# First batch: the order in which pooled keys, v's weights, the last u column and the gate's low parts are made, and the opening of the second stage

## The chip, the cores and the metric

One core of a Trainium2 chip runs the whole program in one launch. The metric is the device time of one execution in microseconds (us). Five engines work side by side, each through a queue of its own in order: TensorE (PE; its weight loads are PEld), VectorE (DVE), ScalarE (ACT), GpSimd (POOL), and SyncE (SP), which issues the DMA transfers.

## The reference

Three layers follow each other, for 8 batches of 576 tokens with 512 features.

```python
k_p = k.reshape(B, H, Sp, 8, D).mean(axis=3); v_p = v.reshape(B, H, Sp, 8, D).mean(axis=3)
x = softmax(q @ k_p.T / sqrt(D)) @ v_p                  # 8 heads of 64, 72 pooled keys
h = gelu_tanh(x @ w_in); u, v = h[..., :512], h[..., 512:]
v_n = (v - mu) / sqrt(var + 1e-6) * g_ln                # per token
x2 = x + (u * (einsum('ts,bsd->btd', w_sg, v_n) + b_sg)) @ w_out
logits = x2 @ w_gate; top 2 of 4 experts, softmax weights
out = sum over the 2 experts of  w * (causal softmax(q k / 8) @ v @ wo)
```

All inputs are float32. The kernel keeps that precision on TensorE by splitting each operand into a high part (rounded to the format fp32r) and a low part (the rest), so that a product is three matmuls: high by high, high by low, low by high.

## The kernel before

The first stage, class PhaseA, takes each batch through pooled attention and the gated layer and writes x2 to DRAM. The second, class PhaseB, starts at 589.7 us of the span and takes each batch through the expert attention.

**First stage, one batch.** Keys and values are pooled by additions (pool_k L171, pool_v). For five tiles of tokens there are scores (sc, L224), the softmax (finish L247 divides by the sum and writes P), transposes (tr) and the product with the values (av). put_x splits the result: high part xh, low part xl, and a plain copy x32 for the sum at the end. Then come the columns of u (upart L407, four of them: U0 to U3), v (Y and V: 48 matmuls and a short fifth tile), the norm of v over its tokens (norm L379: statistics bs and mean and variance mv on VectorE, rs = 1/sqrt on GpSimd in L391 and L392, the high part vnh on ScalarE in L400, the low part vnl on VectorE in L402, for two tiles at a time), the product with w_sg (spatial, tile sp, four columns P0 to P3; L438 multiplies by u, L443 and L445 make the high part gh and the low part gl), and the product with w_out (outp L448, four columns f). L462 adds x32, ScalarE makes x2h and L464 the low part x2l. The two PSUM banks of the tag mm hold the columns of outp in turn, so column f + 2 cannot begin before L464 of column f is done.

**First batch.** It follows an order written by hand, the string SEQ, whose letters name steps in the table of first(). The steps run over a batch whose weights are still being made: W0 to W3 make the columns of w_in for u and W4 to W7 those for v, S0 to S5 those of w_sg, O0 to O3 those of w_out. W and O call load64 (L112), which takes a staged 64-bit load apart into a high and a low part: six VectorE instructions (L124, L125, L127 to L130) and two on ScalarE. load_ws (L156) subtracts the high from the loaded part of w_sg; the string SE says on which engine (P is GpSimd, D is VectorE). Within SEQ batch 1 is begun too: K, Q and o load its keys, its queries and w_out (the last and the raw keys and values share three buffers), k pools its keys, C, X and F are its scores, exponents and finish, R and v load and pool its values. FD lists the pairs (batch, tile) whose finish runs on VectorE, other pairs run on GpSimd. The step "k" before:

```python
def pool_k1():
    with after(4):
        self.pool_k(1)
```

after(4) means behind the finish of tile 4 of batch 0.

Engines take instructions in the order in which the scheduler puts them, which follows SEQ and the dependences. Nothing overtakes on an engine.

**Second stage.** proj makes q and k of a pair of experts in halves (items 00 to 03 are q, q, k, k of the first pair and 10 to 13 of the second), vproj the values (v0 to v4), gate the choice of the experts (g; L796 to L812 on VectorE). run() first does the items of PRE, then goes over units of scores: score (s), three units later trans (t, L886), and between them the items of the table FIRSTF for the first batch, FILL for the others.

Of the kernel before, what the change touches and what calls it, by code (L numbers as in the profile page):

```python
# [17 lines left out]
HS = S // 2  # L18
# [10 lines left out]
AXT = {(0, 0), (0, 2), (0, 4), (1, 0), (1, 2), (1, 3)}  # L29
FD = {(0, 0), (0, 1)}  # L30
XA = (0, 1, 2, 3)
VE = ('PPP', 'PPP')
KE = ('DD', 'PP')
SE = 'PDPP'
SEQ = ("a0 a1 b0 d0 b3 b1 b2 d1 b4 d2 c g p0 h0 h1 p1 h2 h3 s0 e0 f0 s1 e1 f1 s2 s3 e2 f2 e3 f3 "
       "s4 e4 f4 y0 y1 y2 t0 t1 t2 t3 t4 z l W0 U0 W1 U1 W2 U2 W3 U3 K Q k o0 o1 W4 Y0 W5 Y1 W6 Y2 W7 Y3 S2 S1 S0 "
       "V4 N0 S4 N2 S5 N4 S3 C0 C1 o2 O0 P0 C2 X0 X1 F0 o3 O1 P1 C3 F1 X2 O2 R P2 F2 X3 O3 "
       "P3 C4 F3 X4 v")
# [3 lines left out]
class PhaseA:  # L42
# [69 lines left out]
    def load64(self, tv, hi, lo):  # L112
# [16 lines left out]
        nc.vector.scalar_tensor_tensor(lf, zh, 2.0 ** 32, zl, op0=OP.mult, op1=OP.add)  # L129
        nc.vector.scalar_tensor_tensor(lo, lf, 2.0 ** -52, gf, op0=OP.mult, op1=OP.mult)  # L130

    def stage_wi(self, part, j):

        shape, tag = ([128, 2, 4, 128], "ws") if part == 0 else ([128, 2, 512], "wo")
        t = self.w.tile(shape, U64, tag=tag, name="st64", bufs=2)
        for i in range(2):
            k, s = self.wi_cols(part, 2 * j + i)
            self.nc.sync.dma_start(t[:, i], self.ins["w_in"][:, k, s])
            self.STG[part, 2 * j + i] = t[:, i]
# [141 lines left out]
    def av(self, b, steps):  # L281
# [8 lines left out]
        for x in steps:  # L290
# [15 lines left out]
            for p in range(NP):  # L306
                if p in done and "r" in done and (b, p) not in self.X32:
                    self.put_x(b, p, ps[p])

    def put_x(self, b, p, ps):  # L310
# [11 lines left out]
        nc.vector.tensor_sub(fh[:, S:], ps[:, 1, HS - 64:HS], fh[:, 512:S].bitcast(F32))  # L322
        if b == 0 and p in XA:
            nc.scalar.activation(x32, ps[:, :, :HS], AF.Copy)  # L324
        else:
            nc.gpsimd.tensor_add(x32, xh.bitcast(F32), xl.bitcast(F32))
# [80 lines left out]
    def upart(self, b, f):  # L407
# [3 lines left out]
        for h in range(2):  # L411
            s = slice(h * HS, h * HS + HS)
            o = ps[:, h, :HS]
            for kc in range(4):
                xh, xl = self.XH[b, kc][:, s], self.XL[b, kc][:, s]
                nc.tensor.matmul(o, self.wi[0][:, kc, c], xh, start=kc == 0, stop=False)  # L416
                nc.tensor.matmul(o, self.wi[0][:, kc, c], xl, start=False, stop=False)  # L417
                self.upmm = nc.tensor.matmul(o, self.wi[1][:, kc, c], xh, start=False, stop=kc == 3).ins  # L418
# [4 lines left out]
    def spatial(self, b, d):  # L423
# [19 lines left out]
        nc.scalar.activation(gh, u, AF.Copy)  # L443
        eng = nc.vector if d == 3 else nc.gpsimd
        eng.tensor_sub(gl, u, gh.bitcast(F32))  # L445
# [47 lines left out]
    def first(self):  # L493

        done = {}
        def after(i):
            return self.tc.issue_after(done[i]) if i in done else nullcontext()
# [6 lines left out]
        def pool_k1():  # L504
            with after(4):
                self.pool_k(1)
        def load_v1():
# [108 lines left out]
FILL = (('', '12 10 11', '', '13 x0 x1 x2 x3', '', '', 'o3 o1 o0', '', ''), ('v0', 'v1 00 02', '01 o2', '03', '', '', '', 'v2 v3', 'v4 g'))  # L616
FIRSTF = (('10', '11', '12', '13 x0 x1 x2 x3', '', '', '', '', ''), ('v0 00', '', '01 02 v1', '03', '', '', '', 'v2 v3', 'v4 g'))
LASTF = (('', '10 12 11', '', '', '13', '', 'o1', '', 'o0'), ('', '', '', '', '', 'o2', '', '', 'o3'))
SDF = {(0, 0), (0, 1), (0, 5), (0, 8), (1, 0), (1, 2), (1, 7)}
SDL = {(0, 4), (0, 6), (1, 6), (1, 7)}  # L620
PRE = 'v0 00 01 02 03 v1 v2 v3 v4 g'
AVS = [(0, 256), (256, S)]
# [393 lines left out]
```

## Time and profile before

| | us |
|---|---|
| median of 3 runs | 968.65 (967.56 to 971.37) |
| the profiled execution, its own time | 967.84 |
| its span in the trace | 966.1 |
| TensorE busy | 915.0 (95% of the span) |
| VectorE, ScalarE, GpSimd busy | 693.1, 519.0, 447.0 |

The span is counted from the first to the last instruction of the trace, 1.7 us less than the execution's own time. Busy time counts instructions, not register work, and a wait on a semaphore is put down to the instruction that ended it. On the page's 40 slices of 24 us TensorE is at 90% or more in all but the first five, slice 26 and the last. In a row of a time order the first number is the start, the second the duration, and a bracket gives the idle time ahead of it and what ended it.

### The profile page before, as it was taken

How to read it: one execution, taken by the hardware profiler on the slowest of the kernel's cores; microseconds unless marked ns; L12 is line 12 of the kernel's file. 1: busy time of each engine (PE TensorE's matmuls, PEld its weight loads, DVE VectorE, ACT ScalarE, POOL GpSimd, SP SyncE). 2: the span in 40 equal slices, each digit the busy share in tenths (PEclk: the TensorE clock that was granted, in tenths of full speed). 3: DMA queues.
4: the chain of work that ended last, by engine and by line, in shares of the span. 5: the costliest groups of instructions: out<-in, count | busy, mean ns of one | idle time of the engine just before them, and what ended most of it. 6: DMA issues, size and time to landing. Idle time of an engine off the chain costs nothing.

```text
span 966.1 us, 18451 instructions
## 1 busy us (share of the span) xinstructions
PE 915.0 (95%) x6488; PEld 864.4 (89%) x6488; DVE 693.1 (72%) x1869; ACT 519.0 (54%) x1285; POOL 447.0 (46%) x628
## 2 busy tenths in 40 slices
PE   4887699999999999999999999899999999999997
PEld 3677689989989999899899899799999999999987
DVE  6998557757667577577576514897878796878785
ACT  3755334344343343343443433677777777777776
POOL 6545847558369368376583560113222222323221
PEclk9797899999999999999999999999999999999999
DMA  9611522312402404223126014415253534435121
GB/s 326 236 35 44 172 80 82 121 61 71 157 25 81 160 13 140 99 65 132 56 61 191 25 39 134 140 37 176 61 172 88 162 94 147 118 108 163 49 61 75
DMA packets 51644, 102.86 MB, mean 106 GB/s; under 512 B 10592, under 2 KB 16736, under 8 KB 50656
## 3 DMA queue, kind: packets, MB, share of 16 engines
q1 hardware_dynamic: 51408, 101.68, 32.9%
q8 instruction: 52, 0.85, 0.4%
q14 instruction: 40, 0.33, 0.1%
q10 hardware_dynamic: 144, 0.00, 0.0%
HBM read 59.72 MB, written 28.31 MB: 91 GB/s over the span
## 4 chain that ended last, share of the span: by engine, by line
PE 63%; DVE 20%; ACT 6%; POOL 5%; issue 3%; DMA 2%; SPq 1%; POOLq 0%; ACTq 0%; DVEq 0%
PE av L906 4%; PE op L457 4%; PE op L458 4%; PE op L459 3%; PE sp L434 3%; PE sp L432 3%; PE sp L433 3%; PE sc L224 3%; PE t L886 3%; DVE vnl L402 3%; PE pj L715 2%; PE pj L713 2%; PE pj L714 2%; DVE vnh L404 2%; DVE bs L388 2%
## 5 line engine op out<-in xcount | busy, mean ns | idle before, releaser
L860 POOL TENSOR_SCALAR pr<-pr,sm,gw 128x128 f32<-128x128 f32 (+3 forms) x119 | 72.7, 612 | 208.1 <-DVE sm L856 140.9
L844 ACT ACTIVATE pr<-s,sm 128x256 f32<-128x256 f32 (+4 forms) x160 | 83.2, 521 | 41.6 <-DVE sm L841 18.0
L432 PE MATMUL sp<-wsh,vnh 128*128 128x288 f32 x256 | 78.8, 309 | 5.0 <-ACT vnh L400 5.0
L458 PE MATMUL op<-g,woh 128*128 128x288 f32 x256 | 77.0, 301 | 6.8 <-POOL g L445 6.8
L457 PE MATMUL op<-g,woh 128*128 128x288 f32 x256 | 78.5, 309 | 0.3 <-DVE x2l L464 0.3
L416 PE MATMUL up<-x,wih 128*128 128x288 f32 x256 | 76.8, 300 | 1.5 <-ACT xu L324 1.5
L433 PE MATMUL sp<-wsh,vnl 128*128 128x288 f32 x256 | 77.0, 301 | 0.0
L434 PE MATMUL sp<-wsl,vnh 128*128 128x288 f32 x256 | 76.6, 299 | 0.0
L418 PE MATMUL up<-x,wil 128*128 128x288 f32 x256 | 75.7, 296 | 0.0
L715 PE MATMUL pj<-xbh,wql 128*128 128x288 f32 x256 | 75.5, 295 | 0.0
L713 PE MATMUL pj<-xbh,wqh 128*128 128x288 f32 x256 | 75.5, 295 | 0.0
L714 PE MATMUL pj<-xbl,wqh 128*128 128x288 f32 x256 | 75.5, 295 | 0.0
L459 PE MATMUL op<-g,wol 128*128 128x288 f32 x256 | 75.3, 299 | 0.0
L417 PE MATMUL up<-x,wih 128*128 128x288 f32 x256 | 75.1, 293 | 0.0
L841 DVE CUSTOM_DVE_ANT_0 s<-s,mk 128x512 f32<-128x512 f32 (+3 forms) x128 | 62.4, 487 | 3.5 <-PE t L886 2.9
L224 PE MATMUL sc<-kbd,qt 128*128 128x144 f32 (+1 forms) x320 | 50.8, 306 | 14.2 <-DMA qt<-q_in 8.4
L891 DVE TENSOR_TENSOR pbl<-t,pbh 128x512 fp32r<-128x512 f32 (+3 forms) x128 | 60.7, 484 | 3.4 <-ACT pbh L890 1.7
L886 PE MATMUL t<-ident,pr 128*128 128x128 f32 x320 | 57.7, 280 | 4.8 <-POOL pr L860 2.6
L224 PEld LDWEIGHTS sc<-kbd,qt 128*128 128x128 f32 (+1 forms) x320 | 44.4, 192 | 18.3 <-issue 11.1
L906 PE MATMUL av<-pbh,vt 128*128 128x320 f32 (+4 forms) x224 | 55.6, 278 | 2.4 <-ACT pbh L890 2.4
L400 ACT ACTIVATE vnh<-vg,rs 128x512 fp32r<-128x512 f32 (+1 forms) x40 | 27.3, 717 | 54.9 <-POOL rs L392 43.0
L464 POOL TENSOR_TENSOR x2l<-x2l,x2h 128x576 fp32r<-128x576 f32 x8 | 11.4, 1430 | 97.1 <-ACT x2h L463 97.1
(247 smaller groups left out, 3352.8 us busy)
## 6 DMA issues: line engine op xcount, KB each, us to landing
kraw<-k_in SPq DMA_DIRECT2D x16, 576.0 KB, 3.8
x<-x2h SPq DMA_DIRECT2D x32, 288.0 KB, 2.1
x<-x2l SPq DMA_DIRECT2D x32, 288.0 KB, 2.1
xbl<-x SPq DMA_DIRECT2D x32, 288.0 KB, 4.1
xbh<-x SPq DMA_DIRECT2D x32, 288.0 KB, 4.0
kd<-scr SPq DMA_DIRECT2D x64, 144.0 KB, 2.5
out<-o SPq DMA_DIRECT2D x32, 288.0 KB, 3.7
vraw<-v_in SPq DMA_DIRECT2D x16, 512.0 KB, 4.3
```

Source lines behind the costliest of these rows:

```text
L224: nc.tensor.matmul(ps[:m, p // 2, (p % 2) * 144:(p % 2) * 144 + 144], qt[:, p, o:o + m], kbd[:, p, :], start=p % 2 == 0, stop=True, skip_g ...
L432: nc.tensor.matmul(o, vh[:, k, c], self.ws[0][:, k, s], start=k == 0, stop=False)
L433: nc.tensor.matmul(o, vl[:, k, c], self.ws[0][:, k, s], start=False, stop=False)
L434: nc.tensor.matmul(o, vh[:, k, c], self.ws[1][:, k, s], start=False, stop=False)
L457: nc.tensor.matmul(o, self.wo[0][:, k, c], gh[:, s], start=k == 0, stop=False)
L458: nc.tensor.matmul(o, self.wo[0][:, k, c], gl[:, s], start=False, stop=False)
L459: nc.tensor.matmul(o, self.wo[1][:, k, c], gh[:, s], start=False, stop=k == 3)
L713: nc.tensor.matmul(ps, self.wq[0][:, kc, c], xh[:, s], start=kc == 0, stop=False)
L714: nc.tensor.matmul(ps, self.wq[0][:, kc, c], xl[:, s], start=False, stop=False)
L715: nc.tensor.matmul(ps, self.wq[1][:, kc, c], xh[:, s], start=False, stop=kc == 3)
L886: nc.tensor.transpose(ps[:, j], pt[:, 128 * j:128 * j + 128], self.ident)
L906: nc.tensor.matmul(ps[:, s - lo:], vt[:, j, 2 * p + e].rearrange("p a d -> p (a d)"), t[:, e, j * PTS + s:j * PTS + up], start=j == 0 and ...
```

## The change

The steps W3 and U3 move behind V4, the last part of v; the loads of K, Q and o0 come forward, k and o1 stand behind W3. The step "k" now issues two tiny copies on VectorE behind the last instruction of the load64 call before it (W3's), and the pooling waits for these. All of SE's four subtractions are on VectorE. Two more finishes, of tiles 3 and 4 of batch 1, are on VectorE, and so is the low part gl of column 2 in batch 0. The x32 copies of batch 0 are issued behind all its high parts. upart goes over the rows of w_in as 2, 0, 1, 3. The staged loads of w_in use the two tags by j. The second stage opens with the values and the gate, then k, q, and two items of the second pair.

```diff
@@ -27,14 +27,13 @@
 WOF = 4
 XW = 4 * (640 + S)
 AXT = {(0, 0), (0, 2), (0, 4), (1, 0), (1, 2), (1, 3)}
-FD = {(0, 0), (0, 1)}
-XA = (0, 1, 2, 3)
+FD = {(0, 0), (0, 1), (1, 3), (1, 4)}
 VE = ('PPP', 'PPP')
 KE = ('DD', 'PP')
-SE = 'PDPP'
+SE = 'DDDD'
 SEQ = ("a0 a1 b0 d0 b3 b1 b2 d1 b4 d2 c g p0 h0 h1 p1 h2 h3 s0 e0 f0 s1 e1 f1 s2 s3 e2 f2 e3 f3 "
-       "s4 e4 f4 y0 y1 y2 t0 t1 t2 t3 t4 z l W0 U0 W1 U1 W2 U2 W3 U3 K Q k o0 o1 W4 Y0 W5 Y1 W6 Y2 W7 Y3 S2 S1 S0 "
-       "V4 N0 S4 N2 S5 N4 S3 C0 C1 o2 O0 P0 C2 X0 X1 F0 o3 O1 P1 C3 F1 X2 O2 R P2 F2 X3 O3 "
+       "s4 e4 f4 y0 y1 y2 t0 t1 t2 t3 t4 z l W0 U0 W1 U1 W2 U2 K Q o0 W4 Y0 W5 Y1 W6 Y2 W7 Y3 S2 S1 S0 "
+       "V4 W3 k o1 N0 U3 S4 N2 S5 N4 S3 C0 C1 o2 O0 P0 C2 X0 X1 F0 o3 O1 P1 C3 F1 X2 O2 R P2 F2 X3 O3 "
        "P3 C4 F3 X4 v")
 TOK = [(i * 128, min(128, S - i * 128)) for i in range(NT)]
 
@@ -127,12 +126,12 @@
         nc.vector.tensor_scalar(g, a, 0xFF800000, None, op0=OP.bitwise_and)
         nc.vector.tensor_scalar(zh, zh, 0x1FF, None, op0=OP.bitwise_and)
         nc.vector.scalar_tensor_tensor(lf, zh, 2.0 ** 32, zl, op0=OP.mult, op1=OP.add)
-        nc.vector.scalar_tensor_tensor(lo, lf, 2.0 ** -52, gf, op0=OP.mult, op1=OP.mult)
+        self.cv = nc.vector.scalar_tensor_tensor(lo, lf, 2.0 ** -52, gf, op0=OP.mult, op1=OP.mult).ins
 
     def stage_wi(self, part, j):
 
-        shape, tag = ([128, 2, 4, 128], "ws") if part == 0 else ([128, 2, 512], "wo")
-        t = self.w.tile(shape, U64, tag=tag, name="st64", bufs=2)
+        shape = [128, 2, 512] if part else [128, 2, 4, 128]
+        t = self.w.tile(shape, U64, tag=("ws", "wo")[j], name="st64", bufs=2)
         for i in range(2):
             k, s = self.wi_cols(part, 2 * j + i)
             self.nc.sync.dma_start(t[:, i], self.ins["w_in"][:, k, s])
@@ -306,6 +305,8 @@
             for p in range(NP):
                 if p in done and "r" in done and (b, p) not in self.X32:
                     self.put_x(b, p, ps[p])
+        for p in range(NP if b == 0 else 0):
+            self.nc.scalar.activation(self.X32[b, p], ps[p][:, :, :HS], AF.Copy)
 
     def put_x(self, b, p, ps):
         nc, w = self.nc, self.w
@@ -320,9 +321,7 @@
         nc.scalar.activation(xh, ps[:, :, :HS], AF.Copy)
         nc.vector.tensor_sub(xl, ps[:, :, :HS], xh.bitcast(F32))
         nc.vector.tensor_sub(fh[:, S:], ps[:, 1, HS - 64:HS], fh[:, 512:S].bitcast(F32))
-        if b == 0 and p in XA:
-            nc.scalar.activation(x32, ps[:, :, :HS], AF.Copy)
-        else:
+        if b:
             nc.gpsimd.tensor_add(x32, xh.bitcast(F32), xl.bitcast(F32))
         self.X32[b, p], self.XH[b, p], self.XL[b, p] = x32, fh, fl
 
@@ -411,9 +410,9 @@
         for h in range(2):
             s = slice(h * HS, h * HS + HS)
             o = ps[:, h, :HS]
-            for kc in range(4):
+            for kc in (2, 0, 1, 3):
                 xh, xl = self.XH[b, kc][:, s], self.XL[b, kc][:, s]
-                nc.tensor.matmul(o, self.wi[0][:, kc, c], xh, start=kc == 0, stop=False)
+                nc.tensor.matmul(o, self.wi[0][:, kc, c], xh, start=kc == 2, stop=False)
                 nc.tensor.matmul(o, self.wi[0][:, kc, c], xl, start=False, stop=False)
                 self.upmm = nc.tensor.matmul(o, self.wi[1][:, kc, c], xh, start=False, stop=kc == 3).ins
         u = self.XU[b][:, (4 + f) * S:(5 + f) * S].rearrange("p (a n) -> p a n", a=2)
@@ -441,7 +440,7 @@
         part = lambda i: self.GG[b][:, i * S:i * S + S]
         gh, gl = (part(i).rearrange("p (a n) -> p a n", a=2) for i in (d, 4 + d))
         nc.scalar.activation(gh, u, AF.Copy)
-        eng = nc.vector if d == 3 else nc.gpsimd
+        eng = nc.vector if d >= (3 if b else 2) else nc.gpsimd
         eng.tensor_sub(gl, u, gh.bitcast(F32))
         self.G[b, d] = (part(d), part(4 + d))
 
@@ -502,8 +501,10 @@
             with after(PV[i]):
                 self.pool_v(0, (i,))
         def pool_k1():
-            with after(4):
-                self.pool_k(1)
+            with self.tc.issue_after(self.cv):
+                for t in self.RAW["k", 1].values():
+                    self.nc.vector.tensor_copy(t[:, 0, 0, :2], t[:, 0, 0, :2])
+            self.pool_k(1)
         def load_v1():
             for i in range(3):
                 self.load_v(1, i)
@@ -614,11 +615,11 @@
 ALV = 1
 KDM = 1
 FILL = (('', '12 10 11', '', '13 x0 x1 x2 x3', '', '', 'o3 o1 o0', '', ''), ('v0', 'v1 00 02', '01 o2', '03', '', '', '', 'v2 v3', 'v4 g'))
-FIRSTF = (('10', '11', '12', '13 x0 x1 x2 x3', '', '', '', '', ''), ('v0 00', '', '01 02 v1', '03', '', '', '', 'v2 v3', 'v4 g'))
+FIRSTF = (('', '12', '', '13 x0 x1 x2 x3', '', '', '', '', ''), ('v0 00', '', '01 02 v1', '03', '', '', '', 'v2 v3', 'v4 g'))
 LASTF = (('', '10 12 11', '', '', '13', '', 'o1', '', 'o0'), ('', '', '', '', '', 'o2', '', '', 'o3'))
 SDF = {(0, 0), (0, 1), (0, 5), (0, 8), (1, 0), (1, 2), (1, 7)}
 SDL = {(0, 4), (0, 6), (1, 6), (1, 7)}
-PRE = 'v0 00 01 02 03 v1 v2 v3 v4 g'
+PRE = 'v0 v1 v2 v3 v4 g 02 03 00 01 10 11'
 AVS = [(0, 256), (256, S)]
```

On GpSimd, where batch 1's keys are pooled and the first norm follows (kraw and kbd are the raw and pooled keys, wsl the low part of w_sg, rs the norm's factor), before:

```order
L176 TENSOR_TENSOR kraw<-kraw 128x576
L177 TENSOR_TENSOR kraw<-kraw 128x288
L180 TENSOR_TENSOR kbd_96<-kraw 64x2x72 x2
L176 TENSOR_TENSOR kraw<-kraw 128x576
L177 TENSOR_TENSOR kraw<-kraw 128x288
L180 TENSOR_TENSOR kbd_96<-kraw 64x2x72 x2
L163 TENSOR_TENSOR wsl<-st_630,wsh 128x576
L163 TENSOR_TENSOR wsl<-st_638,wsh 128x576
L163 TENSOR_TENSOR wsl<-st_704,wsh 128x576
L391 TENSOR_SCALAR rs<-mv 128x2
L392 TENSOR_TENSOR rs<-rs,mhalf 128x2
```

and with the change:

```order
L259 TENSOR_TENSOR P<-e,st 64x4x16 x2
L175 TENSOR_TENSOR kraw<-kraw 128x576 x2
L176 TENSOR_TENSOR kraw<-kraw 128x288 x2
L179 TENSOR_TENSOR kbd_96<-kraw 64x2x72 x4
L390 TENSOR_SCALAR rs<-mv 128x2
L391 TENSOR_TENSOR rs<-rs,mhalf 128x2
L390 TENSOR_SCALAR rs<-mv 128x2
L391 TENSOR_TENSOR rs<-rs,mhalf 128x2
```

(In the first stage a line of the change has a number one lower, in the second one higher.) The three subtractions of wsl are gone from between the pooling and rs. What stands ahead of rs is now the pooling, which waits for the tiny copies on VectorE.

On VectorE, from the last w_out weights (st and wol are the parts of the load) past the gate's last low part (g), before:

```order
L129 SCALAR_TENSOR_TENSOR st_803<-st_803 128x512
L438 TENSOR_TENSOR xu<-sp,xu 128x576
L130 SCALAR_TENSOR_TENSOR wol<-st_803,g_925 128x4x128
L253 TENSOR_SCALAR st<-st 128x8
L254 RECIPROCAL st<-st 128x8
L229 TENSOR_REDUCE st<-sc 128x8
L232 TENSOR_SCALAR st<-st 128x8
L438 TENSOR_TENSOR xu<-sp,xu 128x576
L253 TENSOR_SCALAR st<-st 128x8
L254 RECIPROCAL st<-st 128x8
L445 TENSOR_TENSOR g<-xu,g 128x576
L229 TENSOR_REDUCE st<-sc 64x8
```

and with the change:

```order
L127 TENSOR_SCALAR st_805<-st_805 128x512
L228 TENSOR_REDUCE st<-sc 64x8
L128 SCALAR_TENSOR_TENSOR st_805<-st_805 128x512
L444 TENSOR_TENSOR g<-xu,g 128x576
L129 SCALAR_TENSOR_TENSOR wol<-st_805,g_927 128x4x128
L236 TENSOR_TENSOR e<-sc,st 64x576
L252 TENSOR_SCALAR st<-st 128x8
L276 TENSOR_TENSOR ptl<-tr,pth 128x4x128
L253 RECIPROCAL st<-st 128x8
L251 TENSOR_REDUCE st<-e 64x8
L256 TENSOR_TENSOR P<-e,st 128x512
L259 TENSOR_TENSOR P<-e,st 128x4x16 x2
```

The last wol stood seven instructions ahead of g, between two multiplications by u (xu); now it follows g. Behind it come the multiplications of P for tile 3, which GpSimd did.

On VectorE at the opening of the second stage (vt, vs are the values, lg to gw the gate, qs the queries and keys, s the scores), before:

```order
L786 TENSOR_TENSOR vt_6025<-vp,vt_6025 128x4x64
L787 COPY lg_6027<-vp 128x4
L772 TENSOR_TENSOR vs<-vp,vs 128x260
L832 ISA s_6252,sm<-s_6252,mk 128x256
L832 ISA sm 128x1
L776 COPY lg_6027<-vs 64x4
L834 ISA s_6248,sm<-s_6248,mk,sm 128x320
L834 ISA sm 128x1
L796 TENSOR_REDUCE gs<-lg_6027 128x5
L799 TENSOR_TENSOR ga<-lg_6027 128x80
L797 TENSOR_TENSOR gg<-lg_6027,gs 128x20
L800 TENSOR_TENSOR ga<-lg_6027 128x80
```

and with the change:

```order
L787 TENSOR_TENSOR vt_6027<-vp,vt_6027 128x4x64
L788 COPY lg_6029<-vp 128x4
L787 TENSOR_TENSOR vt_6027<-vp,vt_6027 128x4x64
L788 COPY lg_6029<-vp 128x4
L773 TENSOR_TENSOR vs<-vp,vs 128x260
L777 COPY lg_6029<-vs 64x4
L797 TENSOR_REDUCE gs<-lg_6029 128x5
L800 TENSOR_TENSOR ga<-lg_6029 128x80
L798 TENSOR_TENSOR gg<-lg_6029,gs 128x20
L801 TENSOR_TENSOR ga<-lg_6029 128x80
L802 TENSOR_TENSOR ga<-ga,tri 128x80
L746 TENSOR_TENSOR qs_6009<-pj,scr 128x288
```

The first scores (ISA rows, L832 and L834) stood among the last values and ahead of the gate; with the change the gate follows the values, and all of q and k before the first score follows the gate.

## Rows read from the trace of the kernel before

**Rows 1.** The page, busy time by engine
```profile
PE 915.0 (95%) x6488; PEld 864.4 (89%) x6488; DVE 693.1 (72%) x1869; ACT 519.0 (54%) x1285; POOL 447.0 (46%) x628
```

**Rows 2.** Windows; us, then each engine's busy time, TensorE clock, DMA share, GB/s
```profile
0.00:140.00 140.00, 106.10 (x604) 92.27 (x605) 105.72 (x203) 69.35 (x181) 79.61 (x109) 0.89 0.44 154
...
600.00:640.00 40.00, 35.48 (x254) 33.46 (x254) 31.02 (x123) 25.91 (x80) 4.95 (x8) 0.96 0.43 117
```

**Rows 3.** What TensorE waited for, whole span: us, times, longest
```profile
PE op L458 <- POOL g L445: 6.8, 1, 6.8
PE sp L432 <- ACT vnh L400: 5.0, 2, 2.8
```

**Rows 4.** Time order of GpSimd around the first norm: start, duration, instruction
```profile
70.78 0.63 POOL L391 TENSOR_SCALAR rs<-mv 128x2 f32<-128x2 f32 x1 [7.93 <-DVE mv L390]
71.49 1.66 POOL L392 TENSOR_TENSOR rs<-rs,mhalf 128x2 f32<-128x2 f32 x1
```

**Rows 5.** GpSimd's pooling of keys, by line: ns min/median/max, first and last start
```profile
L176 POOL TENSOR_TENSOR kraw<-kraw x3: 1410/1476/1875, 30.5 to 111.4; 128x576 f32<-128x576 f32 x3
...
L177 POOL TENSOR_TENSOR kraw<-kraw x3: 798/858/1287, 32.4 to 112.9; 128x288 f32<-128x288 f32 x3
...
L180 POOL TENSOR_TENSOR kbd<-kraw x6: 490/520/841, 33.8 to 115.7; 64x144 f32<-64x144 f32 x6
```

**Rows 6.** Weights of the first batch by line, same columns
```profile
L127 DVE TENSOR_SCALAR g<-a x12: 413/416/1659, 27.1 to 94.4; 128x512 uint32<-128x512 uint32 x12
...
L125 DVE SCALAR_TENSOR_TENSOR a<-st,g x12: 671/680/1567, 26.4 to 91.2; 128x512 uint32<-128x512 uint32 x12
...
L163 POOL TENSOR_TENSOR wsl<-st,wsh x3: 1479/1679/6882, 48.9 to 56.0; 128x576 fp32r<-128x576 f32 x3
```

**Rows 7.** Time order of VectorE, end of v's weights and norm
```profile
64.32 0.68 DVE L130 SCALAR_TENSOR_TENSOR wil<-st,g 128x512 fp32r<-128x512 f32 x1
...
83.12 0.75 DVE L404 SCALAR_TENSOR_TENSOR vnh<-vg,rs,vnh 64x512 fp32r<-64x512 f32 x1
```

**Rows 8.** Windows of the first batch, columns as in rows 2
```profile
54.20:70.00 15.80, 14.04 (x58) 10.20 (x57) 15.80 (x32) 9.29 (x14) 6.88 (x1) 1.00 0.00 1
...
100.80:111.00 10.20, 2.41 (x19) 1.90 (x17) 3.90 (x8) 3.95 (x17) 9.66 (x19) 0.82 0.40 118
111.00:114.00 3.00, 3.00 (x12) 3.00 (x13) 0.00 (x0) 0.00 (x0) 2.92 (x5) 0.50 1.00 365
```

**Rows 9.** Time order of VectorE, last gate column and output projection
```profile
100.54 0.76 DVE L438 TENSOR_TENSOR xu<-sp,xu 128x576 f32<-128x576 f32 x1 [0.28 <-PE sp L436]
102.93 0.17 DVE L253 TENSOR_SCALAR st<-st 128x8 f32<-128x8 f32 x1 [1.64 <-ACT e L234]
...
103.51 0.76 DVE L445 TENSOR_TENSOR g<-xu,g 128x576 fp32r<-128x576 f32 x1 [0.16 <-ACT g L443]
...
114.93 0.77 DVE L462 TENSOR_TENSOR op<-op,xu 128x576 f32<-128x576 f32 x1 [5.08 <-PE op L459]
...
126.12 0.76 DVE L462 TENSOR_TENSOR x2l<-op,xu 128x576 f32<-128x576 f32 x1 [0.83 <-PE op L459]
```

**Rows 10.** Time order of GpSimd, pooling of values and the late gate column
```profile
88.37 1.30 POOL L191 TENSOR_TENSOR vraw<-vraw 128x512 f32<-128x512 f32 x1 [8.54 <-DMA vraw<-v_in]
...
109.51 1.40 POOL L445 TENSOR_TENSOR g<-xu,g 128x576 fp32r<-128x576 f32 x1
```

**Rows 11.** Windows at the beginning of the second stage, columns as in rows 2
```profile
589.70:603.80 14.10, 14.10 (x112) 14.10 (x113) 4.78 (x15) 5.87 (x16) 1.44 (x1) 1.00 0.38 103
603.80:611.40 7.60, 7.39 (x55) 7.07 (x54) 7.12 (x32) 6.21 (x18) 0.73 (x1) 1.00 0.15 34
611.40:620.40 9.00, 4.86 (x30) 3.70 (x30) 8.10 (x37) 5.78 (x19) 2.08 (x4) 0.94 0.91 254
```

**Rows 12.** What TensorE waited for between 600 and 640 us
```profile
PE t L886 <- POOL pr L860: 1.9, 3, 0.9
PE t L886 <- DVE sm L855: 1.4, 1, 1.4
```

## The prediction

> **What bounds the kernel.** I read the page first: TensorE is busy for 95% of the span [rows 1]. So time can be won only where it stands idle or runs at a low clock, and the windows say where that is. In the first 140 us it is busy for 106.1, at a mean clock of 0.89, which leaves 33.9 us idle; between 600 and 640 us it is busy for 35.5, which leaves 4.5 [rows 2]. In the other 786 us it is busy for 773 (915.0 less these two), so 13 us are left there, part of them the tail. The change touches the two stretches with the holes and no other.
>
> The waits name the causes in the first stretch: 6.8 us once, when outp waits for a low part of the gate that GpSimd makes, and 5.0 us in two pieces, when spatial waits for the norm [rows 3]. Everything below is about what VectorE and GpSimd do ahead of these two waits, in time order.
>
> **The change, part by part.**
>
> *Pooled keys in front of the norm.* Before, the first factor rs is done at 71.49 + 1.66 = 73.15, and GpSimd had been idle for 7.93 us ahead of it [rows 4]. Now the pooling of batch 1 stands there and waits for W3's last instruction. That price is eight instructions; by the medians 2 x 1.48 + 2 x 0.86 + 4 x 0.52 = 6.8 us, by the minima 6.4, by the maxima 9.7 [rows 5]. When can it begin? Before, the last low part of w_in ends at 64.32 + 0.68 = 65.0 [rows 7]. VectorE still does the same eight loads; it gains three subtractions of wsl, each about the 0.76 us of a 128x576 subtraction there [rows 9], so 2.3 more. It loses the company of GpSimd's three, which ran up to 6.88 us long while a VectorE instruction of 0.42 us took up to 1.66 and one of 0.68 up to 1.57 [rows 6]. With nothing given back the end is 67.3; with twice the 2.3 given back it is 62.7. I take 64, nearer the low end, since in 54.2 to 70 VectorE was busy for the whole 15.80 us and GpSimd's only work there was that one slow instruction [rows 8]. Then 64 + 0.3 for the copies + 6.8 + 1.5 for rs (it took 0.63 + 1.66 against a busy VectorE, which now has little queued there) = 72.6, so 0.6 earlier than before. The ends are 62.7 + 6.4 + 0.8 = 69.9 and 67.3 + 9.7 + 2.3 = 79.3; both sides stay open, from -3 to +6. TensorE waits for this in either case: moving W3 and U3 behind v brings v's matmuls forward and U3's back, with no matmul added or removed, and the idle time moves to just ahead of spatial.
>
> The rows on GpSimd and VectorE slowing each other invite a rule. The Trainium skill (SBUF — State Buffer, section "SBUF: two separate sides") calls the port pair that the two share an exclusive lock: whichever of a VectorE instruction with two SBUF inputs and a GpSimd instruction starts first has it for the whole instruction. By that rule a pooling instruction would lose at most one VectorE instruction, some 0.7 us, so 5.6 us over eight and rs at about 78 if VectorE always had one ready, and nothing where it is idle. The row of 6.88 us is longer than 1.48 and one such turn, so it speaks for a worse case than the rule does.
>
> *Nothing for two parts.* x32 behind the high parts: on ScalarE's queue the copies of batch 0 stand in the same order as before, so this moves nothing. The order 2, 0, 1, 3 in upart changes which row of w_in comes first, not the number of matmuls, and the first column still waits for its PSUM bank; zero, or a few tenths of gain.
>
> *The gate's low part and the w_out loads.* Before, outp stops for 6.8 us [rows 3] because column 2's low part stands on GpSimd behind the pooling of batch 1's values, which runs from 88.37 on, and ends only at 109.51 + 1.40 = 110.9 [rows 10]. In 100.8 to 111 TensorE is busy for 2.41 us and VectorE for 3.90 [rows 8]. Now VectorE makes that part, and two loads of w_out that came ahead of the norm come behind it. So the last low part on VectorE, which ended at 103.51 + 0.76 = 104.27 [rows 9], is pushed by two loads and one subtraction. A load is three instructions of 0.42 and three of 0.68, 3.3 us, and 2.8 where they overlap by 0.08 each [rows 6]; so 5.6 + 0.7 = 6.3. Against it VectorE's idle time ahead of that point fills up, 0.28 + 1.64 + 0.16 = 2.1 [rows 9], the earlier norm gives 0.6, and GpSimd's pooling of values moves behind, which I put at 1.4, half as much again as the one L125 lost against its median, 1.57 - 0.68 = 0.9 [rows 6]. So 104.27 + 6.3 - 2.1 - 0.6 - 1.4 = 106.5, and outp starts again 4.4 earlier than 110.9. Behind that, two finishes go to VectorE, each about 0.8 + 0.4 us: one ahead of the first sum L462, one ahead of the low part of x2 that frees the bank. One of them shows (1.2), the other fills a gap, of which VectorE had 5.08 us ahead of the first sum [rows 9]. A stop at half clock costs too: in 111 to 114 TensorE does 12 matmuls in 3.00 us [rows 8], 0.25 each; I expect the same again, 0.4 more since fewer matmuls are left for it to slow. The end of outp, 126.12 before [rows 9], comes 4.4 - 1.2 - 0.4 = 2.8 earlier. The ends: -6 when the other 1.5 of contention and more of the norm come back as well; +3 when no contention is given back (1.4), both finishes show (1.2 more) and the norm comes 3.3 late.
>
> *The second stage.* Ahead of the first score now stand two more halves of q (24 matmuls at 0.13, as 112 matmuls take 14.10 us) [rows 11], so it comes 3.1 later; no matmul is added. What was in its way later is out of it: in 603.8 to 620.4 VectorE is busy for 15.2 of 16.6 us, and TensorE is idle for 4.1 of the last 9.0 [rows 11]. The gate and q's subtractions leave that stretch for the one before, in which VectorE is busy for only 4.78 of 14.10. The best case is that all idle time goes, -4.1; the worst that the chain from score to transpose keeps its length and begins 3.1 later, +3.1. Of the waits there, 1.4 us are put down to VectorE and 1.9 to GpSimd [rows 12]; I take the first alone, -1.4.
>
> The sum: -2.8 - 1.4 = -4.2. The profiled execution took 967.84, so 963.6; the median stands 0.8 above it, so **964.4** for the median. This case's own range, with the norm 1 us either way and the second stage from -3 to 0, is 961.5 to 967.5.
>
> **Rivals.**
> - *Faster by far.* The values' pooling no longer slows VectorE at all, and all idle time of the second stage goes: -6 - 4.1 = -10, so 958.5. For it: VectorE's 15.2 of 16.6 busy. Against it: 1.9 us of waits there are GpSimd's [rows 12].
> - *No change.* VectorE becomes the bound that GpSimd was, and part of the change doesn't do what it says, as x32's order shows. The low part comes at 109.5 instead of 106.5, outp ends as before, and the later first score eats the second stage's gain: 968.
> - *Slower.* GpSimd's pooling is starved while VectorE works off the norm's statistics, as L163 was. VectorE has some 5 us of work queued then, seven instructions of about 0.75 [rows 7], so 64 + 0.3 + 5 + 6.4 + 1 = 76.7, 3.6 later than before. The last low part comes at 106.5 + 0.6 + 3.6 + 1.4 = 112.1, past 110.9; the sum and the bank follow later still, and outp ends 2.3 later, 1.2 by this and 1.1 by TensorE's low clock after the longer stop; with +3.1 from the second stage that is +5.4, or 974. It decides from about 75.5 for the first rs on. The row of 6.88 speaks for it; against it, VectorE's queue runs dry then. The Trainium skill's lock (same page and section) is the mechanism, with fewer turns lost than this.
>
> **How the numbers follow.** Half a percent of the median is 4.84 us, about what a measurement of this kernel can tell from no change. The forecast has 0.52, the large gain 0.15, no change 0.22, slower 0.11. More than 4.84 faster is the large gain and a little over half of the forecast, whose centre lies 0.6 short of the bound and whose lower half is fed by two open gains: 0.43. Slower by as much is the third rival and 0.01 besides: 0.12. The rest is 0.45. The range takes in the middle of the large gain and the bulk of the slower case: 957.5 to 973.0.
>
> **What would show it.** The first rs ends between 71.5 and 73.5. The wait of outp for GpSimd's g is gone, and in its place stands a shorter one, 2 to 5 us, for VectorE. The last sum of outp begins at 122 to 124.5 rather than 126.12. The second stage's first score is some 3 us later against its first matmul, and the waits of t there shrink below 3 us. The forecast is wrong if the first rs ends after 75, if outp waits for a P or for pooled values on GpSimd, or if the second stage's transposes begin later and wait as long.

## The result and the profile after

| | median us | ratio to before, 95% interval |
|---|---|---|
| before (7 runs) | 968.65 | |
| with the change (7 runs) | 975.27 | 1.0058, 1.0043 to 1.0074 |

The change makes the kernel slower, by 6.6 us. The forecast was 964.4 and the range ended at 973.0. The profiled execution took 977.19 us with a span of 975.4, the longest of the seven, so its trace shows 1.9 us more than the median, while that of the kernel before shows 0.8 less.

Where the time goes is read from two marks, the first projection of batch 1 (vp) and the first instruction of the second stage. The first, in the time order of TensorE of the kernel before and of the changed one (start, duration, instruction):

```profile
132.18 0.47 PE L355 MATMUL vp<-wih,x 128*128 128x512 f32 x1 [0.17 <-DVE x L322]
```

```profile
141.38 0.40 PE L354 MATMUL vp<-wih,x 128*128 128x512 f32 x1
```

It comes 9.2 us later. The second stage begins at 598.4 instead of 589.7, 8.7 later, and the span is 9.3 longer. So nearly the whole loss of the trace lies in the first batch. The page's busy times and the windows, as in [rows 1, 2]:

```profile
PE 922.8 (95%) x6488; PEld 872.4 (89%) x6488; DVE 695.0 (71%) x1881; ACT 519.2 (53%) x1285; POOL 431.9 (44%) x618
```

```profile
0.00:140.00 140.00, 105.20 (x565) 92.49 (x566) 104.38 (x208) 66.33 (x177) 61.42 (x96) 0.83 0.44 154
600.00:640.00 40.00, 35.20 (x254) 33.88 (x253) 28.01 (x108) 23.09 (x70) 4.32 (x8) 0.96 0.43 119
```

In 140 us TensorE is as busy as before, at a lower mean clock (0.83 for 0.89) and with 39 fewer matmuls done. Its waits over the whole span:

```profile
PE sc L223 <- POOL kbd L179: 2.8, 1, 2.8
...
PE op L456 <- DVE x2l L463: 2.7, 2, 2.4
...
PE av L295 <- DVE x2l L461: 2.4, 1, 2.4
PE op L456 <- DVE xu L437: 1.9, 1, 1.9
...
PE sp L431 <- ACT vnh L399: 1.6, 2, 1.1
```

The wait for g on GpSimd [rows 3] is gone, as forecast, and that of spatial for the norm fell from 5.0 us to 1.6. Four others have come or grown, one for the pooled keys and three for VectorE. Two of these, for x2l, lead to a place that the prediction does not mention. First GpSimd at the norm, to be read against [rows 4]:

```profile
64.04 2.82 POOL L175 TENSOR_TENSOR kraw<-kraw 128x576 f32<-128x576 f32 x2 [33.24 <-DVE kraw L506]
66.82 2.44 POOL L176 TENSOR_TENSOR kraw<-kraw 128x288 f32<-128x288 f32 x2
69.22 2.14 POOL L179 TENSOR_TENSOR kbd<-kraw 64x144 f32<-64x144 f32 x4
71.45 0.23 POOL L390 TENSOR_SCALAR rs<-mv 128x2 f32<-128x2 f32 x1
71.77 0.71 POOL L391 TENSOR_TENSOR rs<-rs,mhalf 128x2 f32<-128x2 f32 x1
```

GpSimd was idle for 33 us, then pools for 7.3 us, and rs ends at 72.48, 0.7 earlier than before. Later GpSimd makes a low part of the gate and begins to pool batch 1's values:

```profile
94.32 1.43 POOL L444 TENSOR_TENSOR g<-xu,g 128x576 fp32r<-128x576 f32 x1 [2.33 <-ACT g L442]
...
102.30 1.76 POOL L190 TENSOR_TENSOR vraw<-vraw 128x512 f32<-128x512 f32 x1 [1.51 <-DMA vraw<-v_in]
```

Then VectorE, against [rows 9]:

```profile
94.34 1.69 DVE L126 TENSOR_SCALAR g<-a 128x512 uint32<-128x512 uint32 x1
...
102.82 1.27 DVE L252 TENSOR_SCALAR st<-st 128x8 f32<-128x8 f32 x1
...
106.34 0.74 DVE L437 TENSOR_TENSOR xu<-sp,xu 128x576 f32<-128x576 f32 x1
...
109.33 0.74 DVE L444 TENSOR_TENSOR g<-xu,g 128x576 fp32r<-128x576 f32 x1
...
115.78 0.73 DVE L461 TENSOR_TENSOR op<-op,xu 128x576 f32<-128x576 f32 x1
...
125.45 0.77 DVE L461 TENSOR_TENSOR op<-op,xu 128x576 f32<-128x576 f32 x1 [2.56 <-PE op L458]
...
133.47 0.76 DVE L461 TENSOR_TENSOR x2l<-op,xu 128x576 f32<-128x576 f32 x1 [3.42 <-DMA x<-x2h]
```

The last xu comes 5.8 us later than the 100.54 of before, the last low part of the gate ends at 110.07, and the first sum of outp is 0.9 later. TensorE itself was not late there. It takes up outp again 3.8 us earlier than before; the first row is of the kernel before, the others are of the changed one:

```profile
110.96 0.61 PE L458 MATMUL op<-g,woh 128*128 128x288 f32 x1 [6.81 <-POOL g L445]
```

```profile
107.14 0.58 PE L456 MATMUL op<-g,woh 128*128 128x288 f32 x1 [1.94 <-DVE xu L437]
...
119.05 0.58 PE L456 MATMUL op<-g,woh 128*128 128x288 f32 x1 [2.43 <-DVE x2l L463]
```

By 114.3 it has done 48 matmuls of outp, two columns; the kernel before had not finished its first by then. The sums and low parts that free the two banks stand in VectorE's queue among the finishes of batch 1, so TensorE, but for transposes, waits until 119.05. The last sum is then 7.3 later, and it waits for a DMA: the store of an earlier part of x2, whose buffer it needs. SP's issues, first of the kernel before, then of the changed one, show why the store is late:

```profile
103.48 4.71 SPq L58 DMA_DIRECT2D kraw<-k_in  x2
108.28 0.38 SPq L71 DMA_DIRECT2D vraw<-v_in  x1
...
116.21 0.33 SPq L71 DMA_DIRECT2D vraw<-v_in  x1
116.59 0.43 SPq L466 DMA_DIRECT2D x<-x2h  x1
```

```profile
119.03 0.80 SPq L57 DMA_DIRECT2D kraw<-k_in  x2
120.64 0.33 SPq L70 DMA_DIRECT2D vraw<-v_in  x1
121.02 0.70 SPq L465 DMA_DIRECT2D x<-x2h  x1
...
128.09 0.33 SPq L70 DMA_DIRECT2D vraw<-v_in  x1
128.46 0.43 SPq L465 DMA_DIRECT2D x<-x2h  x1
```

Of the four loads of batch 2's keys and values, three went out 8 us or more ahead of the first store. Now the first of them goes out 2 us ahead of it, and the fourth stands between two stores, at 128.09, until GpSimd has pooled batch 2's keys and so freed its buffer.

### The profile page after: what moved, and what is told of

The parts are those of the page before. It is cut to its first block, busy times and chain, and to the rows that moved or that the text cites. A ratio compares the mean times of both kernels' runs of the same rounds, so it can differ in the third digit from the quotient of the medians.

```text
span 975.4 us, 18453 instructions
## 1 busy us (share of the span) xinstructions
PE 922.8 (95%) x6488; PEld 872.4 (89%) x6488; DVE 695.0 (71%) x1881; ACT 519.2 (53%) x1285; POOL 431.9 (44%) x618
## 4 chain that ended last, share of the span: by engine, by line
PE 62%; DVE 19%; ACT 6%; POOL 5%; DMA 4%; issue 3%; SPq 1%; POOLq 0%; ACTq 0%; DVEq 0%
PE av L907 4%; PE sc L223 4%; PE op L456 3%; PE sp L431 3%; PE sp L432 3%; PE sp L433 3%; PE op L457 3%; PE op L458 3%; DVE vnl L401 3%; PE t L887 2%; PE pj L714 2%; PE pj L716 2%; PE pj L715 2%; DVE vnh L403 2%; DVE bs L387 2%
## 5 line engine op out<-in xcount | busy, mean ns | idle before, releaser
L275 ACT ACTIVATE pth<-tr 128x640 fp32r<-128x640 f32 (+1 forms) x40 | 26.2, 654 | 57.8 <-PE tr L274 48.2
```

## Experiments

Each kernel was timed in rounds with the kernel before on the same chip. "Below the change" sets its median against the 975.27 of the change, which was timed apart; the kernel before had medians from 968.34 to 969.70 in these sessions, so such a difference is good to about 1 us.

Two things limit what one trace says. The first u column of batch 0 begins at 41.4 to 42.8 us in the five traces of the kernel before and of kernels made from it, none of whose edits acts that early, so a mark compared between two traces is good to about 1 us too. And behind the first stall of the second stage the granted clock falls in some traces and not in others (see the last section); from the second stage's first matmul to the end took 377.0 us in the trace of the change and 374.0 in that of the first experiment.

The common edit "loads behind" is this one:

```diff
-                self.load_k(n + 1)
-                self.load_v(n + 1, 0)
+                if b:
+                    self.load_k(n + 1)
+                    self.load_v(n + 1, 0)
...
                 self.outp(b, f)
+            if b == 0:
+                with self.tc.issue_after(self.put):
+                    self.load_k(n + 1)
+                    self.load_v(n + 1, 0)
```

where self.put is the last store of outp.

### Four parts apart

**Keys pooled freely**, in the changed kernel:

```diff
-            with self.tc.issue_after(self.cv):
...
-            self.pool_k(1)
+            with after(4):
+                self.pool_k(1)
```

> The changed kernel with the pooling of batch 1's keys set free again (behind finish of tile 4, without the tiny copies); the rest of the change stays. Theory A (late keys keep the three raw buffers, so w_out's loads, batch 1's values, batch 2's keys and, on SP's queue behind them, the stores of x2 all come late): 5 to 7 us below the changed kernel, about 969; the first GpSimd pooling of values begins before 95 instead of 102.3, and the last sum of outp does not wait for a store. Theory B (VectorE simply has too much to do after the norm): 0 to 1 us below it, about 974.5.

Measured: 968.03 us, ratio 0.9995 (0.9982 to 1.0009), 7.2 below the change. The size is theory A's, its mechanism is not: the pooling of values begins at 98.84, only 3.5 earlier, and the last sum still waits 1.95 us for a store. What moved on VectorE is the norm, and the wait for the pooled keys is gone:

```profile
66.99 1.21 POOL L390 TENSOR_SCALAR rs<-mv 128x2 f32<-128x2 f32 x1 [27.36 <-DVE mv L389]
68.28 0.71 POOL L391 TENSOR_TENSOR rs<-rs,mhalf 128x2 f32<-128x2 f32 x1
```

With nothing in front of it rs ends at 68.99, 3.5 before the 72.48 of the change, and everything on VectorE up to the first sum moves by that amount (112.34 for 115.78), in the same order. The first projection of batch 1 moves by 5.0. In the trace, 3.0 more come from the second stage, where the clock held here, so the 7.2 are not the keys' alone.

**Finishes back**, in the changed kernel:

```diff
-FD = {(0, 0), (0, 1), (1, 3), (1, 4)}
+FD = {(0, 0), (0, 1)}
```

> The changed kernel with the finishes of tiles 3 and 4 of batch 1 back on GpSimd. Theory A: 0 to 2 us below the changed kernel, about 974, since the stores still come late. Theory B: 3 to 5 us below it, about 971; the first sum of outp begins 2 to 3 us before 115.78.

Measured: 972.76, ratio 1.0040 (1.0027 to 1.0052), between the two theories. The first sum begins 1.5 earlier, at 114.25, and the low part that frees its bank 2.1 earlier, at 116.05; then the third x2h waits 3.5 us for a store.

**The gate's column alone**, in the kernel before:

```diff
-        eng = nc.vector if d == 3 else nc.gpsimd
+        eng = nc.vector if d >= (3 if b else 2) else nc.gpsimd
```

> The kernel before with one part of the change alone: column 2's low part of batch 0 on VectorE. Both theories: the wait of 6.8 us goes, since VectorE was idle there; 4 to 6 us below the kernel before, 963 to 965.

Measured: 967.08, ratio 0.9983 (0.9974 to 0.9991): 1.7 of the 6.8 us. Both theories miss. The first sum comes 3.5 earlier (111.45), but the low part of the third column is held up by ScalarE, which waits 1.5 us for a store:

```profile
122.40 0.76 DVE L464 TENSOR_TENSOR x2l<-op,x2h 128x576 fp32r<-128x576 f32 x1 [1.52 <-ACT x2h L463]
```

**One load of values behind the stores**, in the changed kernel (in middle(), batch 2's; self.put is kept as in the common edit):

```diff
-                self.load_v(n, 1)
+                with self.tc.issue_after(self.put) if b == 1 else nullcontext():
+                    self.load_v(n, 1)
```

> The changed kernel with one load of batch 2's values issued on SP behind batch 0's stores of x2 instead of between them. Theory A: the last sum of outp loses its wait of 3.4 us for a store and av its 2.4, so 3 to 5 us below the changed kernel, about 971.5. Theory B: no difference, 975.

Measured: 972.67, ratio 1.0039 (1.0024 to 1.0053), 2.6 below the change. The last sum no longer waits for a store, but ScalarE's x2h still waits 3.4 us for one.

### The second stage, the sequence, three undone, the low parts

**The second stage alone**, in the kernel before (of FIRSTF the first list alone differs):

```diff
-FIRSTF = (('10', '11', '12', '13 x0 x1 x2 x3', '', '', '', '', ''),
+FIRSTF = (('', '12', '', '13 x0 x1 x2 x3', '', '', '', '', ''),
...
-PRE = 'v0 00 01 02 03 v1 v2 v3 v4 g'
+PRE = 'v0 v1 v2 v3 v4 g 02 03 00 01 10 11'
```

> The kernel before with the second stage's new opening alone (PRE and FIRSTF). From the first projection to the end took 376.4 us in the kernel before and 373.9 to 374.9 in three runs with the new opening, but 377.0 in the profiled run of the changed kernel. Theory C: the opening is worth 2 us, so 966.5. Theory D: it is worth nothing and the three runs differ for another reason, 968.7.

Measured: 968.73, ratio 0.9999 (0.9988 to 1.0010): theory D. Its profiled execution, 972.26 us, is the longest of the twelve; the last section shows the clock falling in it.

**Sequence back**, in the changed kernel:

```diff
-       ... W2 U2 K Q o0 W4 Y0 ...
-       V4 W3 k o1 N0 U3 S4 ...
+       ... W2 U2 W3 U3 K Q k o0 o1 W4 Y0 ...
+       V4 N0 S4 ...
...
-            with self.tc.issue_after(self.cv):
...
-            self.pool_k(1)
+            with after(4):
+                self.pool_k(1)
```

> The changed kernel with the hand-written sequence and the free pooling of batch 1's keys of before; low parts of w_sg, finishes, gate column, copies and second stage stay changed. Theory N (the loss is in the sequence: pooling in front of the norm's factor, and with W3 behind v two loads of w_out behind the norm): 963 to 965, below the kernel before. Theory B (VectorE's added work, low parts, finishes, gate column, is the loss): 968 to 970.

Measured: 965.30, ratio 0.9963 (0.9948 to 0.9977): 0.3 above theory N's range and 10 us below the change. VectorE's added work is not the loss: low parts, finishes and gate column are all still in this kernel.

**Three undone**, in the changed kernel: the edits of the first, second and fourth experiment (keys pooled freely, finishes back, one load of values behind the stores) together.

> The changed kernel with three things undone together: keys pooled freely, the two finishes on GpSimd, batch 2's value load behind the stores; W3 and the last u column stay behind v. If the three losses measured apart (7.2, 2.5, 2.6) add up, 963. If the store's wait and the finishes only hurt because the keys are late, 966 to 968.

Measured: 968.78, ratio 1.0000 (0.9986 to 1.0015), above both expectations: they don't add up. The first sum is now at 108.45, but x2h of the third column waits 4.8 us for a store, and the transposes behind it 4.2.

**Low parts back**, in the changed kernel:

```diff
-SE = 'DDDD'
+SE = 'PDPP'
```

> The changed kernel with three low parts of w_sg back on GpSimd. Theory N: they run against VectorE while it makes v's weights, and stand ahead of the pooling: the first rs ends 1 to 3 us after 72.5 and the time is 976 to 978. Theory B: VectorE is relieved, 973.

Measured: 974.65, ratio 1.0060 (1.0048 to 1.0072). rs ends 3.2 later (1.8 of it stood there at the first u column already, 43.38 for 41.57),

```profile
74.98 0.71 POOL L391 TENSOR_TENSOR rs<-rs,mhalf 128x2 f32<-128x2 f32 x1
```

and yet the time is that of the change. VectorE's order is another one here, and the first sum begins at 113.31, 2.5 earlier than in the change; but then the x2h of the third column waits 4.9 us for a store. So neither a later rs nor an earlier first sum moved the end by as much.

### The loads and the stores

**Loads behind**, in the changed kernel:

> The changed kernel with all of batch 2's loads of keys and values issued behind batch 0's stores of x2. Theory S (what the late keys and values cost at the end of outp is that batch 2's 1.7 MB of raw loads now meet the stores, whose landing rose from 2.8 to 5.2 us in the middle and which free the buffers of x2's parts): the waits of ScalarE and VectorE for a store go, batch 1's first projection begins 4 to 6 us earlier than 141.4, and the time is 970 to 971.5. Rival: the loads were only queued, not in the way, and the one reordered load measured before was all there is to gain, 972.7.

Measured: 968.86, ratio 1.0001 (0.9989 to 1.0013), 6.4 below the change, more than theory S gave it. The first sum stays where it was (115.73), no wait for a store is left, and the last sum comes 5.2 earlier and batch 1's projection 7.0:

```profile
128.31 0.76 DVE L461 TENSOR_TENSOR x2l<-op,xu 128x576 f32<-128x576 f32 x1 [0.83 <-PE op L458]
```

```profile
134.37 0.47 PE L354 MATMUL vp<-wih,x 128*128 128x512 f32 x1 [0.17 <-DVE x L323]
```

The DMA rows around these stores (KB each, us from issue to landing, medians), of the kernel before, the change, and this kernel:

```profile
x<-x2h SPq DMA_DIRECT2D x4, 288.0 KB, 2.9
```

```profile
kraw<-k_in SPq DMA_DIRECT2D x2, 576.0 KB, 6.0
x<-x2h SPq DMA_DIRECT2D x4, 288.0 KB, 5.1
```

```profile
x<-x2h SPq DMA_DIRECT2D x4, 288.0 KB, 2.1
```

**Sequence and finishes back**, in the changed kernel (the diffs of these two above), first without and then with the loads behind:

> The changed kernel with the sequence, the free pooling and the two finishes of before; low parts of w_sg, gate column, copies and second stage stay changed. Theory F (the finishes on VectorE stand ahead of outp's sums in any order): 2 us below the kernel with the sequence back, 963. Rival: they only hurt where GpSimd's values come late, no difference, 965.

> As the kernel before this one in the list, and batch 2's raw loads behind batch 0's stores. Theory S: stores land sooner, but here the waits for them were small, so 0 to 2 us below that kernel, 962 to 964.

Measured: 967.85 (ratio 0.9987, 0.9978 to 0.9997) and **959.90** (0.9912, 0.9894 to 0.9929). Both theories miss the first: with the finishes back it is 2.6 slower than with the sequence back alone. The second comes out below its range. The traces of these two kernels are alike up to the third sum, and then ScalarE's x2h of that column shows the difference, first without, then with the loads behind:

```profile
121.76 0.65 ACT L462 ACTIVATE x2h<-op 128x576 fp32r<-128x576 f32 x1 [6.82 <-DMA x<-x2h]
```

```profile
117.07 0.65 ACT L462 ACTIVATE x2h<-op 128x576 fp32r<-128x576 f32 x1 [1.87 <-issue]
```

With the sequence back alone the first sum begins at 112.81 and no x2h waits for a store; here it begins at 109.36 and x2h waits 6.8 us. What outp had gained it lost against its stores. The second of these kernels is the fastest measured, 8.9 us below the kernel before.

**The change's sequence, keys free, finishes back, loads behind:**

> The changed sequence (W3 and the last u column behind v) with free pooling, finishes on GpSimd and batch 2's raw loads behind the stores. Theory S: against the kernel with three things undone, ScalarE's wait of 4.8 us for a store goes, the first projection of batch 1 begins near 130 instead of 134.1, and the time is 964 to 965. Rival: 968.8 as there, and the transposes' wait stays.

Measured: 962.52, ratio 0.9936 (0.9923 to 0.9949). That is below the range of theory S, and batch 1's projection begins at 126.33. So a kernel with W3 and the last u column behind v can be faster than the one before. The order is not free, though. Two pairs of kernels differ in it alone: this one is 2.6 slower than the fastest, and the kernel with the keys pooled freely is 2.7 slower than that with the sequence back.

**The kernel before with the loads behind, and the gate's column with them:**

> The kernel before with batch 2's raw loads issued behind batch 0's stores of x2, nothing else. Theory W (the loads are a wall that the kernel before just clears, because outp stops until 110.96 and its stores begin at 116.6, long after the loads at 103.5 to 108.8): no difference, 968 to 969; the changed kernel lost by running into the wall later. Rival: the meeting of loads and stores costs the kernel before just as much, 962 to 963, and then it is no part of the change's loss.

> The kernel before with the gate's column 2 on VectorE and batch 2's raw loads behind the stores. Theory W: the gate alone gained 1.7 because its earlier outp met the loads (its third low part of x2 waited 1.5 us for ScalarE, which waited for a store); with the loads behind, most of the 6.8 us comes through, 963 to 965. Rival: the rest of the 6.8 us went into the transposes' and scores' waits, which the loads don't touch, 966 to 967.

Measured: 969.15 (ratio 0.9998, 0.9987 to 1.0009) and 965.41 (0.9951, 0.9935 to 0.9967): theory W, the second 0.4 above its range. The kernel before doesn't gain from the edit alone; nothing in its outp waits for a store. The gate's column gains 4.3 with it instead of 1.7.

## Why the prediction was wrong

**The first rs**: right, as far as a mark of one trace tells. 72.6 was forecast and 72.48 measured. The pooling took 7.3 us for 6.8, with VectorE busy for 4.8 of these 7.3. From the lock that the Trainium skill describes (SBUF — State Buffer, "SBUF: two separate sides"), held for a whole instruction by whichever engine starts first, the prediction estimated a loss between nothing and 5.6 us; the trace, with 0.5, lies near the lower end. Wrong was what it was compared with. The step set 72.6 against the 73.15 of the kernel before and booked 0.6 gained; the earlier v had made room for 68.99, and the pooling in front of rs took 3.5 of these 4.2 back. Undoing it was worth 7.2 us, the largest of the single edits, though the clock in the second stage has a part in that.

**The last low part on VectorE**: 106.5 forecast, 110.07 measured. The failing term is the 1.4 of contention given back. VectorE lost more, not less: L126 took 1.69 beside GpSimd's low part of the gate and L252 1.27 beside the pooling of values, in the rows above, against a median of 0.42 [rows 6] and the 0.17 of [rows 9]. Summed from the first xu to the last low part, what instructions took beyond the median of their kind (where that was 0.1 us or more) rose from 3.3 us before to 4.6, so 1.3 more in place of 1.4 less. That is 2.7 of the 3.6 missed; the 0.6 of the earlier norm didn't arrive either, as the first xu began at 86.99 for 86.63. The term's price had been read from an L125 of 1.57 us, which began at 91.21 beside a P of GpSimd (91.19) and not beside the pooling of values. That pooling did not move out of VectorE's way. Its start moved to 102.3 (from the 88.37 of [rows 10]), onto the stretch in which VectorE has no idle time left. The wait for g did go, and a wait of 1.9 for xu took its place, a little less than the 2 to 5 us in the list of signs. With it outp began again at 107.14, 3.8 earlier than before, close to the 4.4 forecast: it did not need that last low part at once.

**The end of outp**: this is the step that failed. It said 2.8 earlier, with ends of -6 and +3; measured is 133.47 against 126.12, so 7.3 later, outside both. The step followed the engines and left out the queue of SP. By the change, the loads through the three raw buffers move: w_out, batch 1's values, batch 2's keys. Batch 2's keys go out at 119.03 instead of 103.48, into the stores of x2, which then land in 5.1 instead of 2.9 us and hold the buffers that the next column's parts need. The late pooling of keys is the smaller part of that: with batch 1's keys pooled freely, batch 2's still go out at 115.60, and with the old sequence too at 105.89. Putting the loads behind the stores gave back 6.4 us, and in the trace 5.2 of the last sum's 7.3. A second term was too small: of the two finishes one was to show, at 1.2 us, and the other to fill a gap, but the low part that frees the first bank came 2.1 earlier without them. The rest of the way from the 3.8 gained at outp's new start to its end is not taken apart. Against the change, the kernel with the loads behind, the keys free and the finishes back is 12.8 us faster, less than the 16.1 of the three edits apart (7.2, 2.5, 6.4).

**The second stage**: 1.4 forecast. From the first projection to the second pair's first score it took 30.7 us before, 29.9 in the changed kernel and 29.5 to 29.8 in the other runs with the new opening, so 0.8 to 1.2 came; the whole execution shows none of it (the second-stage run). One sign of being wrong came true here. The first score stands 3.2 later, as forecast, but the first transpose too begins 1.3 later, 23.0 us into the stage for 21.7, and the transposes wait 4.2 us in all, about as long as before (4.3) and not below 3. Their waits in the changed kernel, to be read against [rows 12]:

```profile
PE t L887 <- POOL pr L861: 2.0, 1, 2.0
PE t L874 <- DVE sm L856: 1.5, 1, 1.5
...
PE t L887 <- DVE pr L861: 0.7, 1, 0.7
```

**Nothing for two parts**: the first u column began at 41.57 for 41.40, within the spread of that mark, so no gain shows, as said.

**The rivals**: the slower one had the sign, not the cause. It needed the first rs past 75.5 and a starved GpSimd; rs came at 72.48. "No change" had the last low part right, 109.5, but not the end of outp. The forecast's time was nearly reached by undoing the sequence (965.30 for 964.4), and "faster by far" nearly (959.90 for 958.5) by moving the loads behind the stores as well; neither kernel is the change.

Not tried: the pooling behind the norm's factor on GpSimd. How the 7.2 us of the early keys divide between the norm, a lighter meeting with the stores and the second stage's clock is known only so far that the norm moved by 3.5, batch 1's projection by 5.0, and the second stage was 3.0 shorter in the one trace of each.

## What to carry to other kernels

A step moved on one engine also moves every load that waits for its buffers, on the issuing queue and in front of whatever stands behind them there; follow the buffer to its next user, and that user's transfer to the stores that it meets. Move loads that nobody waits for yet behind the stores that free buffers, and time it: it was worth 6.4 and 8.0 us here, and nothing in the kernel before, where nothing waited for a store. Compare a moved operation with what the rest of the change would allow in its place, not only with where it stood before. A gain that stops short of what its wait was worth (1.7 of 6.8) is a sign of a second bound just behind the first.

## What the runs showed of the hardware

A GpSimd instruction took three times its length while VectorE was busy without a gap. This is the P of tile 2 in the changed kernel; the same instruction for tile 0 took 1.04, and VectorE was busy for 6.00 us of 108 to 114:

```profile
108.54 3.04 POOL L256 TENSOR_TENSOR P<-e,st 128x512 f32<-128x512 f32 x1
```

The 2.0 us more are as long as three of the VectorE instructions that ran meanwhile (0.67 to 0.74 each, from 108.73 on), not the one turn at most that the prediction allowed a GpSimd instruction to lose.

The granted clock after nearly the same stall differs from trace to trace. The windows of two kernels with the new opening of the second stage (keys free, and the second stage alone), columns as in [rows 2]:

```profile
613.40:618.40 5.00, 3.50 (x28) 3.15 (x27) 4.25 (x20) 4.12 (x16) 1.20 (x2) 1.00 0.69 190
618.40:623.40 5.00, 2.32 (x18) 1.98 (x18) 4.75 (x22) 3.36 (x11) 0.72 (x2) 1.00 1.02 273
623.40:628.40 5.00, 5.00 (x42) 5.00 (x41) 3.67 (x15) 3.22 (x11) 0.92 (x2) 1.00 0.44 157
```

```profile
610.70:615.70 5.00, 3.50 (x28) 3.16 (x27) 4.26 (x20) 4.12 (x16) 1.21 (x2) 1.00 0.70 196
615.70:620.70 5.00, 2.22 (x15) 1.63 (x14) 4.74 (x22) 3.35 (x11) 0.71 (x2) 1.00 0.93 264
620.70:625.70 5.00, 4.32 (x19) 4.15 (x19) 2.40 (x10) 1.77 (x7) 0.93 (x2) 0.51 0.53 163
```

TensorE was busy for 3.50 and 2.2 to 2.3 of the two stretches of 5 us in both; in the third the first kernel keeps the upper level (1.00, 2.4 GHz) and the second falls to the lower (0.51, 1.2 GHz). The same score of the second stage then begins 51.9 us behind the stage's first matmul in the first and 55.8 in the second, a difference of 3.9 us, more than the new opening is worth. Of the twelve traces with the new opening the clock holds at 1.00 there in five and falls in seven; it falls in all four with the old one. To the end the stage takes 374.0 to 375.1 us in these five, 374.5 to 379.8 in the seven and 375.8 to 377.1 with the old opening. What decides it is open: there is one trace of each kernel.
